# A planner that counts TensorE's instructions in blocks of 256, and a batch's sparse work dealt out anew over the dense stages of the batch before it

## The chip, the core and the metric

The kernel runs on one core of one Trainium2 chip. A core has five engines, each with its own queue that is worked off in order: PE (TensorE: matmuls, and the weight loads that go with them, which the profile shows as PEld), DVE (VectorE), ACT (ScalarE), POOL (GpSimd) and SP (SyncE, which here issues most of the DMAs). The metric is the time on the device in microseconds; less is better.

## The reference

Two stages, for 4 batches, 8 heads, 768 tokens, 64 channels a head. The first is attention under a block mask (blocks of 32 tokens), the second a mixture of four causal attention experts on its output, of which each token takes two.

```python
# stage 1: attention under a block mask, 24 blocks of 32 tokens
scores = scale * np.matmul(q, k.transpose(0, 1, 3, 2))
mask = np.abs(blk_i - blk_j) <= 1                          # neighbours
mask = mask | (blk_i == 0) | (blk_j == 0) | (blk_i == 23) | (blk_j == 23)
for qb in range(24):
    for kb in sampled_blocks[qb]:                          # 3 sampled blocks each
        mask[32*qb:32*qb+32, 32*kb:32*kb+32] = True
attn = softmax(np.where(mask, scores, -1e9)); x = attn @ v # heads joined to 512 channels

# stage 2: four causal attention experts, each token takes the two best
logits = x @ w_gate; w = softmax over the 2 largest
for e in range(4):
    q, k, v = x @ wq[e], x @ wk[e], x @ wv[e]
    ye = causal_softmax(scale * q @ k.T) @ v @ wo[e]
    out += (w of e, 0 where e is not taken) * ye
```

## The kernel before, in words

**Sparse work.** A batch's 768 tokens are six tiles of 128 (four blocks of 32 each). A tile's scores need, for each of its blocks, three neighbouring key blocks, the first and the last block and three sampled ones. `gather_keys` (L581) puts the keys side by side in KK with copies on POOL, ACT or DVE; `gather_values` (L631) does it for the values, into `va` and `vb`, by DMA from a copy of V in HBM (`scr`). Of `va` and `vb` there are two buffers each, taken by even and odd tiles in turn, so tile t's gather can start when tile t-2 has been used. The sampled values take 12 DMAs a tile on SP's queue (L695). `tiles` (L783) then does one half of a tile's heads (a "unit"): scores on PE (L811), row maxima on DVE (L818), exponentials on ACT (L823), transposes on PE (L829), the product with the values on PE (L843, 64 matmuls for each of two pairs of heads), normalisation on DVE, transposes (L860) and the split into `xh` and `xl`. The first and last block of queries attend to all keys: `ends` (L712), twice a batch, works on both together.

For the first batch alone, while nothing else can cover it, two short cuts exist. In `apart` tiles (t < NA) the scores read neighbours and end blocks where they lie (L804, twice the matmuls) and no copies of them are made. And the neighbours and end blocks of the values are copied on POOL from V in SBUF (L642); for the tiles named in `dm` the end blocks come by two DMAs instead (`ends_of`, L650), which here go out from ACT's queue.

**Dense work.** `project_v` (PV, L877; six per batch), `gating` (GT), `project_qk` (PQ, L931), then `expert` (E: scores L972 with a mask by a small matmul L965, maxima L983, exponentials L986, transposes L1022, product L1039) for 2 pairs of experts and 6 row tiles, and `project_o` (O, L1053).

**Order.** No engine's order is written out by hand. The function's end (L1084 to L1092) makes a list `seq` of steps: batch b's dense work is merged, evenly spread, with batch b+1's loads and sparse work, in three stages: the first part of the projections (with tiles 4 and 5 of the same batch and the loads of the next), the second part, and the experts. A step's place in `seq` is its priority. The planner (`Plan.run`, L109) then plays all engines forward with costs that the code gives, and each time an engine is free it takes the ready operation of the best priority. Scores come some steps early: `u`, `e` and `g` say how many for tiles, experts and ends. For PE there is one more rule. The matmuls use the array in different shapes (128 by 128, 64 by 32, 128 by 32 and so on), each operation has its `mode`, and a change of shape costs `SWITCH`; so the planner looks up to `near` steps further for a ready operation of the current shape, and `keep` lets it wait a little for one.

PSUM has two score buffers `s` and four others `w`; the copies out of `w` go to ACT or DVE, whichever the planner finds free.

## Time and profile before

| | |
|---|---|
| timed runs | 524.21, 529.8, 531.16 us; median 529.8 us |
| the profiled execution's own time | 534.0 us |
| its span, from first to last instruction | 532.2 us |
| mean granted clock of PE | 0.987 |
| PE busy | 494.0 us, 93% of the span, 8136 matmuls and 8136 weight loads |
| DVE, ACT, POOL busy | 68%, 63%, 33% |
| share of PE in the chain that ended last | 69% |

Of such a profile one reads first which engine is busy nearly all the time, and then where it is not: a row of the time line with `[2.03 <-issue]` says that the engine stood idle for 2.03 us before this instruction and that nothing which the profile shows (a semaphore, a DMA) released it. In a table by windows each row is a stretch of the span with the busy time of each engine, its instructions, PE's granted clock, and how busy the 16 DMA engines were. The prediction shows the lines.

### The profile page before, as it was taken

To read this page: it belongs to the slowest core of one execution; us is meant where nothing else is said; L and a number is where in the kernel's file an instruction comes from. 1 tells how busy PE (TensorE), PEld (TensorE's weight loads), DVE (VectorE), ACT (ScalarE), POOL (GpSimd) and SP (SyncE) were. 2 spreads that over 40 slices of the span, in tenths; PEclk is the share of its full clock that TensorE was granted. 3 is DMA by queue.
4 is the path that set the end of the run, shared out by engine and by line. 5 is a ranking of instruction groups with operands and counts; after the bars stand their busy time and mean duration, and the time that the engine had idled before them with its cause. 6 is when DMAs were issued, how large, how long until landed. Compare 5 with 4: busy or idle time off the path is not lost.

```text
span 532.2 us, 20854 instructions
## 1 busy us (share of the span) xinstructions
PE 494.0 (93%) x8136; PEld 378.4 (71%) x8136; DVE 364.2 (68%) x980; ACT 333.8 (63%) x936; POOL 177.4 (33%) x446
## 2 busy tenths in 40 slices
PE   2888789897999999998999989999999999999996
PEld 1667477685666777886676758878666778878764
DVE  4867972676897764375978864446988875349783
ACT  2677771575677765484867864556777765435653
POOL 2948742443132350441431332332322321002220
PEclk9989999899999999998999999999999999999999
DMA  7664457987611477976600268867720164000011
GB/s 268 186 163 109 108 143 213 299 208 183 153 30 41 119 222 228 257 181 162 160 26 22 80 154 256 260 154 178 188 65 23 42 161 122 16 2 2 23 41 61
DMA packets 58516, 70.64 MB, mean 133 GB/s; under 512 B 17649, under 2 KB 30065, under 8 KB 58417
## 3 DMA queue, kind: packets, MB, share of 16 engines
q1 hardware_dynamic: 53264, 65.88, 45.9%
q10 hardware_dynamic: 5152, 3.42, 2.2%
q8 instruction: 65, 1.06, 0.9%
q14 instruction: 35, 0.28, 0.2%
HBM read 55.92 MB, written 12.81 MB: 129 GB/s over the span
## 4 chain that ended last, share of the span: by engine, by line
PE 69%; DVE 12%; DMA 5%; ACT 4%; issue 3%; POOL 3%; SPq 2%; POOLq 0%; ACTq 0%; DVEq 0%
PE w L943 10%; PE s L972 7%; PE w L843 7%; PE w L1039 7%; PE w L829 7%; PE w L1022 6%; PE s L811 6%; PE w L1053 6%; PE w L886 6%; DVE sm L983 2%; DMA vb<-scr 2%; POOL va L642 2%; PE s L726 2%; PE w L860 2%; DMA KK<-in_kT_dram 2%
## 5 line engine op out<-in xcount | busy, mean ns | idle before, releaser
L1012 POOL TENSOR_SCALAR p<-p,sm 128x512 f32<-128x512 f32 (+3 forms) x73 | 44.6, 621 | 165.6 <-DVE sm L999 46.5
L469 ACT ACTIVATE pt<-w 128x512 f32<-128x512 f32 (+3 forms) x157 | 81.5, 549 | 22.4 <-PE w L829 9.9
L823 ACT ACTIVATE p<-s,sm 128x256 f32<-128x256 f32 x192 | 78.0, 487 | 16.1 <-DVE sm L818 13.0
L986 ACT ACTIVATE p<-s,sm 128x512 f32<-128x512 f32 (+3 forms) x128 | 68.5, 544 | 24.6 <-DVE sm L983 23.8
L610 POOL COPY KK<-KK 128x128 f32 x231 | 58.2, 298 | 50.2 <-PE s L811 32.3
L473 DVE COPY pt<-w 128x512 f32<-128x512 f32 (+3 forms) x83 | 47.0, 577 | 25.7 <-PE w L829 17.5
L983 DVE TENSOR_REDUCE sm<-s 128x2 f32<-128x1024 f32 (+3 forms) x64 | 54.2, 853 | 11.2 <-PE s L972 10.6
L818 DVE TENSOR_REDUCE sm<-s 128x4 f32<-128x1024 f32 x48 | 57.7, 1214 | 5.6 <-PE s L811 4.4
L829 PE MATMUL w<-ident,p 128*128 128x128 f32 x384 | 54.6, 281 | 7.3 <-ACT p L823 3.8
L829 PEld LDWEIGHTS w<-ident,p 128*128 128x128 f32 x384 | 43.6, 143 | 14.6 <-ACT p L823 5.0
L843 PE MATMUL w<-vb,pt 128*32 128x65 f32 x1536 | 49.5, 220 | 2.9 <-DMA vb<-scr 1.8
L843 PE MATMUL w<-va,pt 128*32 128x65 f32 x1536 | 49.8, 223 | 2.3 <-issue 2.3
L1022 PE MATMUL w<-ident,p 128*128 128x128 f32 x336 | 49.1, 280 | 2.6 <-DVE p L1011 0.9
L972 PE MATMUL s<-qk 64*128 64x512 f32 (+3 forms) x256 | 50.4, 491 | 0.0
L1022 PEld LDWEIGHTS w<-ident,p 128*128 128x128 f32 x336 | 36.7, 141 | 16.9 <-issue 7.9
L1039 PE MATMUL w<-pt,vb 128*64 128x128 f32 x672 | 46.0, 279 | 2.8 <-issue 2.1
L1039 PEld LDWEIGHTS w<-pt,vb 128*64 128x64 f32 x672 | 36.1, 137 | 16.5 <-issue 6.7
L843 PEld LDWEIGHTS w<-va,pt 128*32 128x32 f32 x1536 | 36.6, 109 | 15.4 <-issue 8.6
L943 PE MATMUL w<-xh,wqkh 128*128 128x512 f32 (+1 forms) x128 | 45.6, 356 | 0.3 <-issue 0.3
L811 PE MATMUL s<-KK,q 64*32 64x256 f32 x1280 | 44.4, 382 | 0.3 <-ACT p L823 0.3
L596 ACT ACTIVATE KK<-KK 128x256 f32<-128x256 f32 (+3 forms) x84 | 34.5, 458 | 15.4 <-DMA KK<-in_kT_dram 10.5
L943 PE MATMUL w<-xl,wqkh 128*128 128x512 f32 (+1 forms) x128 | 43.5, 340 | 0.0
(132 smaller groups left out, 996.9 us busy)
## 6 DMA issues: line engine op xcount, KB each, us to landing
vb<-scr SPq DMA_DIRECT2D x270, 65.0 KB, 3.1
va<-scr SPq DMA_DIRECT2D x12, 780.0 KB, 6.2
scr<-VN SPq DMA_DIRECT2D x12, 520.0 KB, 5.4
KK<-in_kT_dram SPq DMA_DIRECT2D x16, 384.0 KB, 5.9
out_dram<-ws SPq DMA_DIRECT2D x24, 256.0 KB, 2.3
ws<-in_v_dram SPq DMA_DIRECT2D x18, 256.0 KB, 3.3
q<-in_qT_dram SPq DMA_DIRECT2D x18, 256.0 KB, 4.9
va<-scr SPq DMA_DIRECT2D x6, 585.0 KB, 5.8
```

What stands on the lines that cost most here:

```text
L469: nc.scalar.activation(dst(), src(), AF.Copy, scale=1.0 if mul is None else mul)
L610: e.tensor_copy(dst, src)
L811: nc.tensor.matmul(s.t[32 * g:32 * g + 32, j, 256 * i:256 * i + 256], q.t[r, pairs[i], 32 * g:32 * g + 32], kg.t[r, i, cl(t, g)].rearrange ...
L823: pl.add("ACT", 0.37, lambda i=i, j=j, n=n: nc.scalar.activation(pp.t[:, 256 * n:256 * n + 256], s.t[:, j, 256 * i:256 * i + 256], AF.Exp, ...
L829: nc.tensor.transpose(w.t[:, 128 * c:128 * c + 128], pp.t[:, 512 * (c // 2) + 256 * i + 128 * (c % 2):][:, 0:128], ident)
L843: nc.tensor.matmul(o.t[32 * g:32 * g + 32, VW * n:VW * n + VW], pt.t[:, 4 * i + 2 * j + c, 32 * g:32 * g + 32], x.t[:, cl(t, g), h * VW:h ...
L943: nc.tensor.matmul(w.t[:, 0:cw], a[:, k, x], y[:, k, c0:c0 + cw], start=n == 0, stop=n == 3 * KT - 1)
L972: nc.tensor.matmul(ss[i].t[:, j, 0:cw], qk.t[x, 0, r * 128:(r + 1) * 128], qk.t[x, 1, c0:c0 + cw], start=not mask_first, stop=mask_first o ...
L983: pl.add("DVE", 0.09 + 0.00208 * cw, lambda i=i, cw=cw: nc.vector.tensor_reduce(sm.t[:, 2 * i:2 * i + 2], ss[i].t[:, :, 0:cw], AX.X, op=AL ...
L986: pl.add("ACT", 0.26 + 0.00083 * cw, lambda i=i, j=j, c0=c0, cw=cw: nc.scalar.activation(pps[j].t[:, p0[j] + c0:p0[j] + c0 + cw], ss[i].t[ ...
L1022: nc.tensor.transpose(w.t[:, 128 * i:128 * i + 128], pps[j].t[:, p0[j] + 128 * t:][:, 0:128], ident)
L1039: nc.tensor.matmul(o.t[64 * j:64 * j + 64, 0:128], vb.t[:, t, e * D:(e + 1) * D], pts[j].t[:, t0s[j] + t], start=t == 0, stop=t == r, tile ...
```

## The change

Five things change together.

1. The planner gets a model of how PE's instructions arrive: PE operations carry their number of instructions (`ni`), `fetching` counts them in blocks of `BLOCK` = 256 and holds that the next block is asked for when a block begins and is at hand `FETCH` us later, or more when many DMAs are queued (`JAM`). An operation that would be late by it costs that much.
2. PE's choice is made anew: all ready operations within `near` steps of the oldest are gathered; one that costs neither a change of shape nor a late block is taken at once, and else the cheapest, with 0.02 for each step of lower priority. `pull` is 0, so that term does nothing. `keep` is empty: PE no longer waits for an operation of its shape.
3. Scores of experts may come 7 steps early (before 4), of ends 4 (before 5).
4. In the first batch, tile 3 is no longer `apart` (`na` 3 for 4), and no end blocks of values come by DMA (`dm` empty for (1,)): tile 1's eight come by POOL copies.
5. The next batch's sparse work is dealt out anew: its ends and tile 0 stand beside the second part of the projections, tiles 1, 2 and 3 beside the experts. Before, tiles 0 and 1 stood beside the second part, and the ends with tiles 2 and 3 beside the experts.

```diff
 SWITCH, DLAT = 0.095, 1.9
+BLOCK, FETCH, JAM = 256, 3.6, 0.15
...
+        count, at_hand = 63.0, {}
+
+        def fetching(o, d, put=False):
+
+            nonlocal count
+            n, late, c = o.ni * 1.02, 0.0, count
+            asked = {}
+            while n and int((c + n) // BLOCK) > int(c // BLOCK) + len(asked):
+                k = int(c // BLOCK) + len(asked) + 1
+                tb = t + late + d * (k * BLOCK - c) / n
+                w = max(0.0, at_hand.get(k, 0.0) - tb)
+                late += w
+                asked[k + 1] = tb + w + FETCH + min(2.5, JAM * max(0.0, dma_free - t - 1.0))
+            if put:
+                count += n
+                at_hand.update(asked)
+            return late
...
-                    if pick is not None and (x[0][0] > pick[0][0] + self.near or all(m[0] != mode for m in o.mode)):
+                    if pick is not None and x[0][0] > oldest + self.near:
...
+                        if e != "PE":
+                            pick = x
+                            break
+                        c = min(SWITCH * ((m[0] != mode) + (m[0] != m[1])) for m in o.mode) + fetching(o, o.dur[0])
+                        if pick is None:
+                            pick, oldest, ready = x, x[0][0], []
+                        ready.append((c, x))
+                        if c == 0.0:
                             break
                         continue
                     skipped.append(x)
+                if pick is not None and e == "PE":
+                    def rank(y):
+
+                        if y[0] == 0.0:
+                            return -1.0
+                        m = y[1][2].mode[0][0]
+                        return y[0] - self.pull * sum(z[1][2].dur[0] for z in ready if z[1][2].mode[0][0] == m) + 0.02 * (y[1][0][0] - oldest)
+
+                    pick = min(ready, key=rank)[1]
+                    skipped += [y[1] for y in ready if y[1] is not pick]
...
-    TUNE = dict(window=24, look=20, near=3, u=7, e=4, g=5, keep={"PE": 0.09}, byact=0, dm=(1,), wat=2)
+    TUNE = dict(window=24, look=20, near=3, u=7, e=7, g=4, keep={}, byact=0, dm=(), wat=2, na=3, pull=0.0)
...
-    NKG, NQ, NA, NC = 3, 4, 4, 6
+    NKG, NQ, NA, NC = 3, 4, TUNE["na"], 6
...
+    MIX = ([4, 5], ['e', 0], [1, 2, 3])
+
+    def tiles_of(b, x):
+        return sum([{"e": ends_(b), "e0": ends_(b)[:1], "e1": ends_(b)[1:]}[t] if isinstance(t, str) else block(b, t) for t in x], [])
+
...
-        seq += merge(first_part(b), block(b, 4) + block(b, 5), [] if last else loads(b + 1))
+        seq += merge(first_part(b), tiles_of(b, MIX[0] if b else [4, 5]), [] if last else loads(b + 1))
         if not last:
-            seq += merge(second_part(b), block(b + 1, 0) + block(b + 1, 1))
-            seq += merge(experts(b), ends_(b + 1) + block(b + 1, 2) + block(b + 1, 3))
+            seq += merge(second_part(b), tiles_of(b + 1, MIX[1]))
+            seq += merge(experts(b), tiles_of(b + 1, MIX[2]))
```

Beside these, each `pl.add("PE", ...)` gets its `ni`: 16 for an ends' score, 48 for its product, 32 (apart 64) and 64 for a tile's, 24 for PV and PQ, 8 or 12 for an expert's score, 8 for each row tile in its product, 12 for O, 2 for each transpose.

Three places in the orders, before and after. Line numbers of the changed kernel are larger by 36 in the second half of the file. First PE, at the end of batch 1's experts, where tile 3 of batch 2 runs (L811, L860, L829 and L843 are the tile's scores, last transposes, transposes and product; L1022, L1039 and L1053 an expert's transposes, its product, and the output projection). Before:

```order
L811 MATMUL s<-KK,q 32x256 x16
L1022 MATMUL w<-ident,p 128x128 x4
L860 MATMUL w<-ident,xn 128x128 x2
L1022 MATMUL w<-ident,p 128x128 x2
L811 MATMUL s<-KK,q 32x256 x8
L1039 MATMUL w<-pt,vb 64x128 x6
L1022 MATMUL w<-ident,p 128x128 x2
L811 MATMUL s<-KK,q 32x256 x8
L1039 MATMUL w<-pt,vb 64x128 x2
```

After:

```order
L1089 MATMUL w<-woh,o 128x512
L896 MATMUL w<-ident,xn 128x128 x2
L1058 MATMUL w<-ident,p 128x128 x2
L865 MATMUL w<-ident,p 128x128 x4
L1058 MATMUL w<-ident,p 128x128 x2
L865 MATMUL w<-ident,p 128x128 x4
L847 MATMUL s<-KK,q 32x256 x16
L1075 MATMUL w<-pt,vb 64x128 x4
L879 MATMUL w<-va_71,pt 32x65 x4
L879 MATMUL w<-vb_73,pt 32x65 x4
```

Before, operations of three array shapes follow each other in pieces of 2 to 16; now the output projection and the transposes stand together, then the scores, then the tile's product, four rows of which follow on those shown.

Second, PE around the product of batch 2's tile 1 with its gathered values (`va_71` and `vb_73` are the odd tiles' buffers; L972 and L965 are an expert's scores and mask). Before, the end of that product:

```order
L843 MATMUL w<-va_71,pt 32x65 x4
L843 MATMUL w<-vb_73,pt 32x65 x4
L972 MATMUL s<-qk 128x512 x2
L972 MATMUL s<-qk 128x256 x2
L965 LDWEIGHTS ident_b
L965 MATMUL s<-tri,ident_b 128x128
L965 LDWEIGHTS ident_b
L965 MATMUL s<-tri,ident_b 128x128
L860 MATMUL w<-ident,xn 128x128 x2
```

After, its beginning:

```order
L1075 MATMUL w<-pt,vb 64x128 x12
L865 MATMUL w<-ident,p 128x128 x4
L1001 LDWEIGHTS ident_b
L1001 MATMUL s<-tri,ident_b 128x128
L1001 LDWEIGHTS ident_b
L1001 MATMUL s<-tri,ident_b 128x128
L1008 MATMUL s<-qk 128x512 x2
L879 MATMUL w<-va_71,pt 32x65 x4
L879 MATMUL w<-vb_73,pt 32x65 x4
```

Before, the product stands ahead of the first scores of batch 1's experts; now it stands behind scores, masks and a product (L1075) of these experts.

Third, ACT in the first batch, around the exponentials of tile 1 (L823, now L859). Before, with the two DMAs of `ends_of`:

```order
L823 ACTIVATE p<-s,sm 128x256 x4
L469 ACTIVATE pt<-w 128x512
L469 ACTIVATE q<-q 128x512
L469 ACTIVATE pt<-w 128x512
L823 ACTIVATE p<-s,sm 128x256 x2
L653 DMA va_71<-VN 32x4x520
L653 DMA vb_73<-VN 32x4x520
L823 ACTIVATE p<-s,sm 128x256 x2
```

After:

```order
L859 ACTIVATE p<-s,sm 128x256 x4
L632 ACTIVATE KK<-KK 128x4x96
L505 ACTIVATE pt<-w 128x512 x2
L859 ACTIVATE p<-s,sm 128x256 x4
L384 TENSOR_LOAD si
L644 ISA
L644 ACTIVATE KK<-KK 128x4x32
```

The two DMAs are gone from ACT's queue; a static copy of tile 3's keys (L632), and behind the exponentials its sampled keys (`TENSOR_LOAD` into registers and L644, 2 times 3 copies), have come into it.

More of the change, by code (lines that the diff above doesn't have):

```diff
@@ L63, with __init__, add @@
 SWITCH, DLAT = 0.095, 1.9
+BLOCK, FETCH, JAM = 256, 3.6, 0.15
 class Op:
[L67 removed]
+    __slots__ = ("eng", "dur", "fn", "prio", "deps", "outs", "n", "slots", "seq", "end", "unit", "lat", "ready", "mode", "xfer", "done", "nd", "ns", "ni")
 class Plan:
[L74 removed]
+    def __init__(self, window, look, near, lat, keep, pull):
         self.ops, self.writers, self.window, self.look, self.near, self.lat = [], {}, window, look, near, lat
[L76 removed]
+        self.keep, self.pull = keep, pull
         self.now = (0, 0)
[L79 removed]
+    def add(self, eng, dur, fn, r=(), w=(), prio=None, unit=None, xfer=None, nd=1, mode=None, ni=0):
         o = Op()
@@ L271, in f @@
         return ap.bitcast(F32)
-    TUNE = dict(window=24, look=20, near=3, u=7, e=4, g=5, keep={"PE": 0.09}, byact=0, dm=(1,), wat=2)
-    pl = Plan(window=TUNE["window"], look=TUNE["look"], near=TUNE["near"], lat={"PE": 0.22, "ACT": 0.17, "DVE": 0.16, "POOL": 0.15, "SP": 0.1}, keep=TUNE["keep"])
+    TUNE = dict(window=24, look=20, near=3, u=7, e=7, g=4, keep={}, byact=0, dm=(), wat=2, na=3, pull=0.0)
+    pl = Plan(window=TUNE["window"], look=TUNE["look"], near=TUNE["near"], lat={"PE": 0.22, "ACT": 0.17, "DVE": 0.16, "POOL": 0.15, "SP": 0.1}, keep=TUNE["keep"], pull=TUNE["pull"])
     def ring(name, n, shape, dt=F32, space=None, ordered=False):
@@ L860, in tiles @@
         pl.add("PE", 0.22, lambda: [nc.tensor.transpose(w.t[:, 128 * i:128 * i + 128], xn.t[:, i], ident)
-                                    for i in range(2)], r=[xn], w=[w, (X[t // 4], "r")], unit=unit, mode=FULL)
+                                    for i in range(2)], r=[xn], w=[w, (X[t // 4], "r")], ni=4, unit=unit, mode=FULL)
         a = 32 if t == 0 else 0
@@ L1054, in mm @@
                     n += 1
-        pl.add("PE", 1.49, mm, r=[(oo, p) for p in range(EP)] + ["wo"], w=[w, (y, "r")], unit=unit, mode=FULL)
+        pl.add("PE", 1.49, mm, r=[(oo, p) for p in range(EP)] + ["wo"], w=[w, (y, "r")], ni=12, unit=unit, mode=FULL)
         evacuate(512, lambda: y.t, lambda: w.t, [w], [y], unit=unit)
```

40 lines of the change are left out of this document (17 added, 23 removed).

## The prediction

> **What bounds the kernel now.** I read the page first, then the stretches by windows, then PE's own idle times.
>
> ```profile
> span 532.2 us, 20854 instructions
> PE 494.0 (93%) x8136; PEld 378.4 (71%) x8136; DVE 364.2 (68%) x980; ACT 333.8 (63%) x936; POOL 177.4 (33%) x446
> PE 69%; DVE 12%; DMA 5%; ACT 4%; issue 3%; POOL 3%; SPq 2%; POOLq 0%; ACTq 0%; DVEq 0%
> ```
>
> PE is busy 494.0 of 532.2 us and carries 69% of the chain. The work on PE hardly changes, so a reordering can win only from the 38 us in which PE stands, from time at a lower clock, and from changes of array shape.
>
> ```profile
> 25.00:50.00 25.00, 20.78 (x698) 17.32 (x703) 18.68 (x50) 19.63 (x53) 16.51 (x35) 0.93 0.55 137
> 50.00:75.00 25.00, 21.68 (x526) 15.80 (x510) 20.76 (x45) 17.53 (x45) 15.53 (x28) 1.00 0.52 124
> 75.00:100.00 25.00, 22.02 (x230) 17.66 (x234) 8.61 (x21) 10.06 (x23) 8.34 (x15) 0.93 0.72 206
> 100.00:125.00 25.00, 22.71 (x511) 18.26 (x507) 17.86 (x48) 16.96 (x43) 11.62 (x39) 1.00 0.89 236
> 225.00:250.00 25.00, 23.23 (x485) 18.63 (x484) 16.51 (x45) 15.66 (x42) 7.95 (x28) 0.93 0.76 178
> 300.00:325.00 25.00, 22.85 (x390) 17.29 (x389) 14.88 (x45) 17.17 (x52) 10.61 (x31) 0.93 0.66 177
> 350.00:375.00 25.00, 25.00 (x508) 20.77 (x508) 16.37 (x44) 17.27 (x47) 6.83 (x24) 1.00 0.67 163
> 375.00:400.00 25.00, 24.43 (x375) 17.45 (x374) 22.26 (x61) 18.45 (x53) 9.01 (x21) 1.00 0.46 116
> ```
>
> The columns are length, busy time of PE, PEld, DVE, ACT, POOL, then PE's clock, the DMA engines' share, GB/s. Up to 100 us (the first batch) PE misses 3 to 4 us of every 25. Later it is full but for three stretches, and two of those also have a clock of 0.93. What PE waits for, in order of time:
>
> ```profile
> 24.12 0.30 PE L804 MATMUL s<-KK,q 64*32 64x64 f32 x4 [1.09 <-issue]
> 48.69 0.25 PE L843 MATMUL w<-vb,pt 128*32 128x65 f32 x2 [1.16 <-issue]
> 124.14 0.22 PE L843 MATMUL w<-va,pt 128*32 128x65 f32 x1 [2.03 <-issue]
> 243.19 0.27 PE L843 MATMUL w<-vb,pt 128*32 128x65 f32 x2 [0.64 <-DMA vb<-scr]
> 244.59 0.24 PE L843 MATMUL w<-vb,pt 128*32 128x65 f32 x1 [1.13 <-DMA vb<-scr]
> 316.22 0.44 PE L1039 MATMUL w<-pt,vb 128*64 128x128 f32 x4 [2.15 <-issue]
> 346.94 0.50 PE L943 MATMUL w<-xh,wqkh 128*128 128x512 f32 x1 [0.32 <-issue]
> ```
>
> Five of them have no releaser ("issue"): no semaphore, no data. They sit in the middle of an operation. What they share is the count of instructions just before:
>
> ```profile
> q8 instruction: 65, 1.06, 0.9%
> 117.40:121.80 4.40, 4.40 (x140) 3.69 (x128) 3.75 (x9) 4.40 (x13) 2.69 (x11) 1.00 1.09 229
> 309.60:313.80 4.20, 4.20 (x130) 2.82 (x127) 3.45 (x13) 3.67 (x14) 2.89 (x8) 1.00 1.02 223
> 343.40:345.70 2.30, 2.30 (x130) 2.11 (x129) 1.72 (x5) 0.96 (x3) 2.14 (x10) 1.00 1.10 359
> ```
>
> PE's 16272 loads and matmuls, some 2% more with waits, over 65 packets of a queue named "instruction" are 255 to a packet. And the three stretches ahead of the later stalls each hold 257 to 268 loads and matmuls, in 4.4, 4.2 and 2.3 us. From the start of such a stretch to PE's return (124.14, 316.22, 346.94) it took 6.7, 6.6 and 3.5 us, each time with the DMA engines full (share above 1). So I read these stalls as a block of 256 being used up before the next has come.
>
> The Trainium skill, page "Runtime: NRT & Kernel Launch", section "Instruction fetch mechanics", says that instructions are refilled in 16 KiB blocks of 256, and that the cost of crossing a block is mostly hidden. The size agrees with the 65 packets of 1.06 MB. That it is hidden does not agree with 6.4 us of idle time in the rows above; taken at its word it makes the counter worthless, which is the second rival below.
>
> **The change, part by part.** The sum is made against the profiled execution's 534.0 us (span 532.2 and 1.8 around it).
>
> *Blocks, batches 1 to 3.* I went through both orders of PE by 256 instructions with durations from the trace. Before, outside the first batch, blocks of 4.3, 3.7, 4.7, 4.1, 4.1, 2.0 and 3.6 us stand there; the new order has one under 5 us (4.4, near the end, where few DMAs run). The 2.03, 2.15 and 0.32 us go: -4.5 us. Blocks of 5.0 to 5.8 us remain, about ten, under the 6.6 of the crowded cases; if three of them wait 1.2 us each, only -0.9 is left.
>
> *Blocks, first batch.* Before 2.4, 3.1, 2.0, 4.1, 2.5, 3.2, 3.5; now 3.4, 3.1, 2.0, 3.9, 2.7, 4.1, 4.5. Tile 3 sends 128 instructions fewer. Of 1.09 and 1.16 us I take half: -1.1 us (0 to -2.3).
>
> *The gathered values.* Odd buffers of `va` and `vb` were free when batch 1's tile 5 was done at 228.11; then SP had to issue the sampled rows of batch 2's tile 1:
>
> ```profile
> 227.06 1.05 PE w L843 x64
> 231.72 11.30 SPq L695 DMA_DIRECT2D vb<-scr  x12
> vb<-scr SPq DMA_DIRECT2D x270, 65.0 KB, 3.1
> ```
>
> 231.72 + 11.30 is 243.0, and landing comes on top: PE, 14 us after the release, was too early. In the new order the ends, tile 0 and the first expert work stand ahead of that product, and the PE work between the same two points is about 37 us by the trace's durations. The smallest such distance of any tile in batches 1 to 3 rises from 14 to 19 us, against the roughly 15 that SP and the landing take. -1.8 us (0.64 + 1.13). Of the three tiles now beside the experts each still has its 12 DMAs in SP's queue, ahead of outputs that nobody waits for.
>
> *The clock.* Two of the stalls are followed by a stretch at half clock:
>
> ```profile
> 317.70:321.00 3.30, 3.30 (x18) 2.34 (x11) 2.01 (x6) 3.04 (x10) 2.25 (x9) 0.50 0.60 192
> 246.10:249.30 3.20, 3.20 (x16) 2.04 (x13) 2.31 (x4) 0.51 (x2) 0.62 (x1) 0.50 1.10 246
> ```
>
> Half of 3.3 and 3.2 us: -3.2 us when both stalls go. The stall of 2.03 us at 124.14 had no such stretch, so this is not certain to the execution; 0 is the other end.
>
> The Trainium skill, page "TensorE: Matmul & The Clock Gate", section "HAM oscillation — how this bites in real kernels", puts the rule at no PE idle gaps above about 3.4 us. Here the clock fell after 2.15 us; by that rule it should not have, and the sum would be 3.2 us higher (about 523). I go by the rows.
>
> *Changes of shape.* Counted on the orders, neighbouring operations of PE differ in shape 322 times before and 304 times now, though `keep` no longer waits for one. What one costs:
>
> ```profile
> 353.43 1.89 PE s L811 x64
> 421.59 1.02 PE s L811 x32
> ```
>
> The second 32 matmuls cost 0.87, so each run of a shape has about 0.15 us on top. 18 times 0.10 (part of it is the pipeline's own) is -1.8 us; 0.9 to 2.7.
>
> *First batch's copies.* `dm` puts eight more copies on POOL, and tile 3's keys are now laid out:
>
> ```profile
> L642 POOL COPY va<-VN 32x520 f32<-32x520 f32 (+2 forms) x53 | 34.3, 648 | 21.1 <-DVE sm L733 10.0 <-PE w L843 8.5
> 38.23 0.53 POOL L610 COPY KK<-KK 128x128 f32 x2 [5.74 <-ACT p L823]
> 31.98 0.86 ACT L608 ACTIVATE KK<-KK 128x128 f32 x3 [1.90 <-DMA vb<-scr]
> 33.47 0.71 ACT L608 ACTIVATE KK<-KK 128x128 f32 x3 [0.63 <-issue]
> ```
>
> 8 times 0.648 is 5.2 us on POOL, which fits the 5.74 that POOL stood idle just there: nothing, and 5.2 without that cover. Two sampled sets on ACT take 4.1 us with their waits (0.63 + 0.71 + 0.86 + 1.90), with tile 2's last exponentials queued behind, which PE's transposes wait for; POOL and the two DMA issues are freed of as much. ACT has 5.4 us free in 25 to 50 us. I take +1 us; -1 if the saved DMAs count, +4 if all of it shows.
>
> *New waits.* Some are sure to come where none was, ends beside gating for one. I take +1.5 us, about one more wait like those at 243; 0 to 7.
>
> Sum: 534.0 - 4.5 - 1.1 - 1.8 - 3.2 - 1.8 + 1.0 + 1.5 = 524.1 us for an execution like the profiled one. That one is 4.2 us above the median of the timed runs (529.8); taken off, 519.9 us.
>
> What stays: PE's wait of 2.1 us between 75 and 100 us, on the copies of `qk` that stand in ACT's and DVE's queues behind copies of keys whose load has not landed. In the new order as many of these copies stand there.
>
> ```profile
> PE w L829 <- DVE qk L475: 2.1, 1, 2.1
> ```
>
> **The rivals.**
>
> *DVE becomes the bound beside the second part (slower).* The ends' work on DVE, four times:
>
> ```profile
> L733 DVE TENSOR_REDUCE sm<-s 128x2 f32<-128x1024 f32 (+1 forms) x16 | 15.1, 952 | 5.8 <-PE s L726 5.5
> L764 DVE TENSOR_TENSOR ws<-w,sm 128x260 f32<-128x260 f32 x8 | 3.4, 425 | 1.6 <-PE w L754 0.9 <-POOL KK L610 0.7
> L768 DVE TENSOR_TENSOR ws<-ws,sm 128x128 f32<-128x128 f32 x8 | 3.2, 396 | 0.3
> ```
>
> is (15.1 + 3.4 + 3.2) / 4 = 5.4 us a batch, some 7 with the small ones. It moves beside gating, whose result every expert needs. If all of it lay open at the three transitions, with a stretch at half clock each time (1.6): 519.9 + 3 x 8.6 = 546 us. It decides from 3.3 us a transition on, where the 10 us of gain are gone. Against it: DVE has 7 to 9 us free in the stretches of the second part (17.86, 16.51, 16.37 of 25), tile 1's work leaves them, and it is the experts' stretch that is full (22.26 of 25), which gets lighter.
>
> *The stalls without a releaser are not blocks of instructions (little gain).* Then the counter moves them at best: 4.5, 1.1 and 1.6 us of clock stay, 527 us. Against it stand the three counts near 256.
>
> *As many waits come as go.* The planner's costs are its own, and PE's order is fixed before the run. Wherever an exponential or a copy is later than planned, PE stands. With one wait of 243's kind in each of the three batches beyond what I took (1.8 + 1.6 of clock), 530 us: no change.
>
> *More than these stalls goes.* If the first batch loses half of the 3 to 4 us that PE misses in each 25 as well, 8 us less: 512 us.
>
> **How the numbers follow.** Chances: the forecast with its own range, 515 to 525, 0.51; more goes 0.16; as many come as go 0.20; not blocks 0.07; DVE the bound 0.06. The likeliest gives 519.9. The costs' open ends reach from 512 (the last rival, about the lower bounds together) to 530 (the third), and outside 510 to 531 I leave no more than 2 in 10. About 2% is what a measurement of this kernel can tell from no change: below 519.2 is faster. That takes a little under half of the forecast (0.24) and the last rival (0.16), with 0.02 from elsewhere: 0.42. Above 540.4 lies the larger part of the DVE rival: 0.05. The rest, 0.53, is within.
>
> **What would show it.** In the changed kernel's trace: no idle time "issue" above 1 us on PE after 100 us (blocks); no wait of PE for `vb<-scr` in batch 2 (gather); a granted clock of 1.00 in every stretch after 100 us; the stretches 25 to 75 us with PE at 21 to 22 as before (first batch); DVE under 22 of 25 in every stretch. If "issue" stalls stand where blocks are long, the count is wrong; if PE waits for DVE's maxima or gating at the transitions, the first rival is right; if PE's busy time falls by more than 3 us, I have mis-sized the changes of shape.

## The result and the profile after

| | before | changed | ratio (95% interval) |
|---|---|---|---|
| first comparison, median of 4 runs each | 529.3 us | 511.9 us (511.2 to 512.2) | 0.968 (0.962 to 0.975) |
| once more beside the last three experiments, 7 and 4 runs | 527.3 us | 513.3 us (511.9 to 513.5) | 0.974 (0.971 to 0.977) |

The changed kernel is faster by 14 to 17 us. The forecast was 519.9, with 510 to 531 as its range. The profiled execution of the changed kernel took 512.2 us. That of the kernel before took 534.0 us and was one of its slow ones, 4.7 to 6.7 us over the two medians, so what is read below from the two traces (21.8 us between them) is more than the gain of the medians. The changed kernel's page, with the span, the busy times and the shares of the chain of waits:

```profile
span 510.4 us, 20714 instructions
PE 484.3 (95%) x8072; PEld 373.7 (73%) x8072; DVE 372.0 (73%) x992; ACT 327.3 (64%) x936; POOL 183.4 (36%) x450
PE 83%; DVE 9%; ACT 3%; DMA 2%; issue 2%; ACTq 0%; POOL 0%; DVEq 0%; POOLq 0%
```

PE's share of the chain rose from 69% to 83%, and DMA, POOL and SP's queue have nearly left it. The stretches of the changed kernel by windows (length, busy time of PE, PEld, DVE, ACT, POOL, then clock, DMA share, GB/s):

```profile
0.00:75.00 75.00, 55.46 (x1356) 39.39 (x1357) 58.31 (x137) 48.59 (x129) 52.99 (x111) 0.93 0.56 158
25.00:50.00 25.00, 20.07 (x625) 16.00 (x623) 20.91 (x49) 18.71 (x53) 22.91 (x41) 0.93 0.49 122
50.00:75.00 25.00, 21.22 (x500) 14.33 (x499) 21.55 (x46) 19.37 (x55) 16.73 (x30) 0.93 0.51 118
75.00:100.00 25.00, 25.00 (x360) 20.53 (x363) 12.52 (x30) 12.03 (x27) 6.50 (x15) 1.00 0.84 247
125.00:150.00 25.00, 24.90 (x440) 18.03 (x438) 23.53 (x62) 19.32 (x60) 11.09 (x28) 1.00 0.55 139
...
75.00:500.00 425.00, 422.70 (x6686) 330.03 (x6687) 311.22 (x846) 275.58 (x799) 129.53 (x338) 1.00 0.51 135
```

And the kernel before, in the same two parts (up to 75 us, and from there to 10 us before the end):

```profile
0.00:75.00 75.00, 55.79 (x1436) 42.51 (x1436) 54.92 (x135) 46.82 (x118) 45.52 (x103) 0.98 0.59 165
75.00:522.00 447.00, 431.98 (x6656) 331.48 (x6656) 306.68 (x840) 284.25 (x811) 130.56 (x342) 0.99 0.48 129
```

Up to 75 us PE stands 19.2 us before and 19.5 us now: nothing gained there. From 75 us on it stood 15.0 us before and stands 2.3 us now, at full clock throughout. So in these two traces the time came from that part alone, and PE is now full there. Three of the waits that PE still has in the first batch (a wait of 0.80 us at 28.8 and one of 2.62 us for ACT at 34.5 stand beside them), and the kind of wait that comes back in each batch behind it, in the changed kernel's timeline:

```profile
48.93 0.62 PE L847 MATMUL s<-KK,q 64*32 64x256 f32 x2 [0.76 <-issue]
54.56 0.27 PE L879 MATMUL w<-vb,pt 128*32 128x65 f32 x2 [0.82 <-issue]
58.73 0.41 PE L896 MATMUL w<-ident,xn 128*128 128x128 f32 x2 [1.72 <-DVE sm L889]
161.92 0.33 PE L1075 MATMUL w<-pt,vb 128*64 128x128 f32 x2 [0.40 <-DVE pt L509]
```

To split the gain I gave each of PE's operations the time that it takes up to the next one where nothing waits (the same kind of operation followed by the same kind, elsewhere in the two traces). By that measure the work itself went from 466.9 to 464.8 us, and all that lies on top of it (waits and lower clock) from 52.3 to 32.5 us. These two, 2.1 and 19.8 us, make up the 21.8 us between the spans. Every "work" and "on top" below is of this kind, worked out from the traces. The sum is firm, the split is not: with the shortest time of each kind as the measure the work falls by 3.5 us, with the mean of those without idle time behind them by 5.7 us. A plain account of the same two traces is PE's idle time, 12.1 us less; the clock, 1.6 us less lost (13.4 and 10.2 us of PE's busy time lie at half clock); and PE's busy time without the clock's part, 8.1 us less (487.3 and 479.2 us).

### The profile page after: what moved, and what is told of

Read it like the earlier page. It is cut to its first block, busy times and chain, and to the rows that moved or that the text cites. A ratio compares the mean times of both kernels' runs of the same rounds, so it can differ in the third digit from the quotient of the medians.

```text
span 510.4 us, 20714 instructions
## 1 busy us (share of the span) xinstructions
PE 484.3 (95%) x8072; PEld 373.7 (73%) x8072; DVE 372.0 (73%) x992; ACT 327.3 (64%) x936; POOL 183.4 (36%) x450
## 4 chain that ended last, share of the span: by engine, by line
PE 83%; DVE 9%; ACT 3%; DMA 2%; issue 2%; ACTq 0%; POOL 0%; DVEq 0%; POOLq 0%
PE w L979 14%; PE w L879 9%; PE w L865 8%; PE s L1008 8%; PE s L847 8%; PE w L1075 7%; PE w L922 7%; PE w L1058 6%; PE w L1089 6%; PE w L896 2%; PE s L762 2%; DVE sm L854 2%; PE w L780 2%; PE w L790 2%; DMA pt<-in_v_dram 2%
## 5 line engine op out<-in xcount | busy, mean ns | idle before, releaser
L859 ACT ACTIVATE p<-s,sm 128x256 f32<-128x256 f32 x192 | 78.1, 485 | 13.6 <-DVE sm L854 8.2
L1022 ACT ACTIVATE p<-s,sm 128x512 f32<-128x512 f32 (+3 forms) x128 | 68.2, 544 | 27.3 <-DVE sm L1019 21.0
L505 ACT ACTIVATE pt<-w 128x512 f32<-128x512 f32 (+3 forms) x134 | 67.5, 530 | 21.6 <-PE w L865 12.1
L509 DVE COPY pt<-w 128x512 f32<-128x512 f32 (+3 forms) x106 | 63.2, 614 | 24.2 <-PE w L865 17.3
L854 DVE TENSOR_REDUCE sm<-s 128x4 f32<-128x1024 f32 x48 | 58.0, 1215 | 12.7 <-PE s L847 12.4
L879 PE MATMUL w<-va,pt 128*32 128x65 f32 x1536 | 48.6, 224 | 0.3 <-issue 0.3
L879 PE MATMUL w<-vb,pt 128*32 128x65 f32 x1536 | 47.6, 221 | 0.8 <-issue 0.8
L847 PE MATMUL s<-KK,q 64*32 64x256 f32 x1344 | 46.9, 388 | 1.1 <-issue 1.1
L1075 PE MATMUL w<-pt,vb 128*64 128x128 f32 x672 | 43.8, 277 | 1.6 <-DVE pt L509 1.6
L879 PEld LDWEIGHTS w<-va,pt 128*32 128x32 f32 x1536 | 35.5, 110 | 13.1 <-issue 6.4
L1075 PEld LDWEIGHTS w<-pt,vb 128*64 128x64 f32 x672 | 36.1, 137 | 12.2 <-issue 3.2
L678 POOL COPY va<-VN 32x520 f32<-32x520 f32 (+2 forms) x57 | 36.7, 645 | 20.2 <-DVE sm L769 10.1
L979 PE MATMUL w<-xh,wqkl 128*128 128x512 f32 (+1 forms) x128 | 43.3, 339 | 0.0
```

Source lines behind the costliest of these rows:

```text
L505: nc.scalar.activation(dst(), src(), AF.Copy, scale=1.0 if mul is None else mul)
L509: nc.vector.tensor_copy(dst(), src())
L847: nc.tensor.matmul(s.t[32 * g:32 * g + 32, j, 256 * i:256 * i + 256], q.t[r, pairs[i], 32 * g:32 * g + 32], kg.t[r, i, cl(t, g)].rearrange ...
L854: pl.add("DVE", 1.16, lambda: nc.vector.tensor_reduce(sm.t[:, 0:4], s.t.rearrange("p j (t c) -> p (j t) c", t=2), AX.X, op=ALU.max, negate ...
L859: pl.add("ACT", 0.37, lambda i=i, j=j, n=n: nc.scalar.activation(pp.t[:, 256 * n:256 * n + 256], s.t[:, j, 256 * i:256 * i + 256], AF.Exp, ...
L879: nc.tensor.matmul(o.t[32 * g:32 * g + 32, VW * n:VW * n + VW], pt.t[:, 4 * i + 2 * j + c, 32 * g:32 * g + 32], x.t[:, cl(t, g), h * VW:h ...
```

## The experiments

Two kinds of kernel were run: the changed kernel with one part taken back, and the kernel before with one or two parts alone. No run takes back the new choice among ready operations (part 2) by itself, and the leads go together with `keep`. Ratios are against the kernel before, timed beside them (527.6 us for the first four rows of experiments, 526.9 for the mix alone, the counter alone and the shifted ones, 527.3 for the rest).

| kernel | us | ratio (95% interval) | changes of shape | PE idle after 75 us | longest stall without a releaser after 75 us |
|---|---|---|---|---|---|
| before (trace: the execution of 534.0 us) | 529.3 | 1 | 322 | 15.0 | 2.15 |
| changed | 511.9 | 0.968 (0.962 to 0.975) | 304 | 2.3 | none |
| changed, counting off | 517.0 | 0.979 (0.973 to 0.985) | 301 | 5.3 | 2.57 |
| changed, old mix | 532.1 | 1.006 (1.003 to 1.010) | 305 | 17.2 | 3.28 |
| changed, old first batch | 517.5 | 0.981 (0.975 to 0.986) | 303 | 5.8 | 2.34 |
| changed, old leads | 524.6 | 0.996 (0.993 to 0.998) | 312 | 8.7 | 1.76 |
| before, new mix alone | 525.2 | 0.995 (0.992 to 0.998) | 302 | 10.6 | 2.33 |
| before, counter alone | 532.2 | 1.009 (1.005 to 1.013) | 328 | 10.1 | 1.74 |
| before, mix and leads | 520.6 | 0.988 (0.985 to 0.991) | 306 | 8.7 | none |
| before, borders shifted | 530.7 | 1.013 (1.004 to 1.022) | 322 | 14.5 | 2.95 |
| changed, borders shifted | 517.5 | 0.982 (0.977 to 0.987) | 304 | 3.9 | 0.74 |
| changed, once more | 513.3 | 0.974 (0.971 to 0.977) | 304 | 2.5 | none |
| changed, 5.5 us a block, old first batch | 517.2 | 0.982 (0.979 to 0.985) | 304 | 4.3 | none |
| changed, 4.5 us a block | 516.4 | 0.978 (0.974 to 0.982) | 301 | 4.6 | 1.11 |

The idle times are from 75 us to about 10 us before the end. A time over another by more than its row explains is mostly in the clock, in the work itself, or ahead of 75 us.

### Are the stalls blocks of instructions?

The direct test leaves every engine's order as it is and moves only the borders of the blocks, by half a block:

```diff
         def sc(i, c0, cw):
+            for _ in range(32 * (b == 0 and pp_ == 0 and i == 0)):
+                nc.tensor.matmul(ss[0].t[0:64, 0, 0:1], ident[0:64, 0:64], ident[0:64, 0:1], start=True, stop=True, ...)
             for j in range(2):
```

> The kernel before, order of every engine unchanged, with 32 products of one column (128 instructions) ahead of the first score product, which overwrites what they wrote; so every later block border falls half a block earlier in the same work. Blocks theory: the stalls of 2.03, 2.15 and 0.32 us leave the operations at which they stood (the 256 instructions up to each now take 5.5 us and more); new ones, if any, stand where 256 instructions pass in 4.3 to 4.5 us (near 191, 205, 228, 363 and 436 us), all at whole multiples of 256 in the count with 128 more. 525 to 530 us. Rival (the stalls belong to these operations, by their shape or their data): they stay at the same operations, 530 to 533 us with the work added.

The kernel before with its borders shifted, PE's timeline:

```profile
124.14 0.32 PE L846 MATMUL w<-va,pt 128*32 128x65 f32 x1 [2.95 <-issue]
311.37 0.77 PE L1042 MATMUL w<-pt,vb 128*64 128x128 f32 x10
340.83 0.40 PE L946 MATMUL w<-xh,wqkh 128*128 128x512 f32 x1
359.93 0.44 PE L832 MATMUL w<-ident,p 128*128 128x128 f32 x2 [2.05 <-issue]
```

The second and the third row hold the operations ahead of which PE stood 2.15 and 0.32 us (the program's `pt,vb` product and key projection); it now goes through them without a pause. A new stall stands at 359.93, where the order had a stretch of 256 in 4.4 us (forecast: near 363; at the other four places named there is none). In the first batch stalls of 1.68, 1.41 and 1.40 us have come where two of 1.09 and 1.16 us were. The time, 530.7 us, is the rival's number; it is the places that speak against the rival, not the time. The stall near 124 us has the same time by chance, but stands 130 loads and matmuls further on in the program (before at the 4225th, here at the 4483rd, of which 128 are added): again at the end of a block. That a stall would come there was not foretold. I had read 5.5 us for that block off the trace of before, with the old stall of 2.03 us in it; here its 256 instructions take 3.3 us from border to border. The same 128 instructions in the changed kernel:

> The changed kernel with the same 128 instructions ahead, order of every engine unchanged, so that its planner's count is half a block off. Theory A (after 75 us the order has so few dense stretches that the place of the borders hardly matters): 512 to 515 us, with at most one stall of 1 to 2 us near 217 us, where 256 instructions now pass in 2.5 us. Theory B (the count's phase is what keeps the stalls away): 517 us and more, several stalls without a releaser after 100 us.

It took 517.5 us, theory B's number, but after 75 us its trace is that of theory A: one stall above 0.5 us, at the foretold place, but of 0.74 us (219.4). The first batch holds most of the rest: PE has stalls of 1.26, 0.82 and 2.08 us there, and two stretches of 6.8 us at half clock. So with this one shift the changed order after 75 us depends little on where the borders lie, but in the first batch it does.

Over all 14 traces, PE has 36 idle times of 0.6 us and more without a releaser. With PE's loads and matmuls times 1.02, plus 63, over 256 (the planner's own count), 35 of the 36 stand 0.00 to 0.11 above a whole number. In these 35 stalls the 16 KB packet of the queue named "instruction" ends 1.22 to 1.60 us before PE goes on; in the odd one (0.64 us, at 9.25 blocks) 1.96 us. That settles the question for this kernel: PE stands because its next block comes late.

Whether a dense stretch stalls goes with the DMA engines. Three kernels send the same 251 loads and matmuls, in the same order, through the block that ends near 218 us, and all take 2.6 us for it. By windows (the last two columns are the DMA share and GB/s), first the kernel before with mix and leads, no stall behind it:

```profile
215.80:218.40 2.60, 2.60 (x125) 2.43 (x127) 1.08 (x4) 1.20 (x2) 0.00 (x0) 1.00 0.27 74
```

Then the changed kernel with shifted borders, 0.74 us behind it:

```profile
215.70:218.30 2.60, 2.60 (x122) 2.43 (x124) 1.07 (x4) 1.20 (x2) 0.00 (x0) 1.00 0.53 130
```

Then the kernel before with the mix alone, 2.33 us:

```profile
215.50:218.10 2.60, 2.60 (x122) 2.42 (x124) 1.06 (x4) 1.20 (x2) 2.22 (x10) 1.00 1.07 235
```

And two other blocks, of the kernel before with the counter alone, 1.74 us behind the first, none behind the second:

```profile
308.40:311.70 3.30, 3.30 (x127) 2.25 (x134) 2.96 (x8) 2.93 (x12) 1.45 (x6) 1.00 1.01 311
334.50:336.80 2.30, 2.30 (x130) 2.09 (x129) 1.71 (x7) 1.48 (x4) 1.87 (x8) 1.00 0.09 16
```

The same instructions stall not at all with the engines at 0.27, a little at 0.53 and most at 1.07. Read in this way over all traces after 75 us, a block that passed in less than 4.5 us was followed by a stall of 0.3 us or more at 10 of 11 places with a share above 0.97 (at the eleventh PE waited for DVE just then), and at 1 of 37 places with less. No run changed the traffic alone, so these are cases beside each other and not a test.

### What the counter is worth

```diff
-BLOCK, FETCH, JAM = 256, 3.6, 0.15
+BLOCK, FETCH, JAM = 10 ** 9, 3.6, 0.15
```

> The changed kernel with a block so large that none is ever used up, so the planner counts nothing; table and mix as changed. PE's order then differs only in the first batch and at one place near 115 us. Theory A (the counter earned the gain of the first batch's stalls, the mix the rest): stalls without a releaser of 1 us and more come back before 75 us and nowhere else, 513 to 515 us against 511.9. Theory B (the counter is the change, its avoided stalls carry most of the 17 us): over 520 us, with stalls without a releaser after 100 us.

The changed kernel without counting, PE's timeline and the window behind the stall:

```profile
103.39 0.31 PE L879 MATMUL w<-vb,pt 128*32 128x65 f32 x6 [2.57 <-issue]
```

```profile
104.40:107.80 3.40, 3.40 (x22) 2.39 (x15) 2.73 (x5) 1.29 (x4) 2.43 (x7) 0.50 0.62 209
```

5.1 us slower than the changed kernel's first median, 3.7 us slower than its second, and the intervals of the ratio overlap (0.973 to 0.985 against 0.971 to 0.977 for the second); the trace shows what the time alone would not. Neither theory had the place right. The orders differ only up to about 115 us. The counter did not thin out the first batch (0.98 us there without it, 0.76 and 0.82 with it); it took apart one dense stretch beside the second part of batch 0, where the stall and the half clock behind it make 100 to 125 us longer by 4.3 us. The disappeared stalls of 124, 316 and 347 us owe it nothing: they are gone in this kernel too (the largest that is left behind 104 us is 0.42 us, at another border, 315 us).

The counter alone (with the new choice among ready operations), written as the changed kernel with the old table and mix:

```diff
-    TUNE = dict(..., e=7, g=4, keep={}, ..., dm=(), ..., na=3, ...)
+    TUNE = dict(..., e=4, g=5, keep={"PE": 0.09}, ..., dm=(1,), ..., na=4, ...)
-    MIX = ([4, 5], ['e', 0], [1, 2, 3])
+    MIX = ([4, 5], [0, 1], ['e', 2, 3])
```

> The kernel before with the counter and the new choice among ready operations alone; old table, old mix. 328 changes of shape instead of 322. Theory A (with the old mix the counter can't get round the dense stretches: 256 instructions still pass in 2.0 and 3.4 us at two places): 526 to 531 us, the wait for vb<-scr and the 2.1 us wait stay. Theory B (the counter is what takes the stalls away): 519 to 523 us, no stall without a releaser over 1 us after 100 us.

PE's timeline:

```profile
314.02 0.37 PE L847 MATMUL s<-KK,q 64*32 64x256 f32 x1 [1.74 <-issue]
```

532.2 us, no gain and a little loss (0.9%): theory A's side, 1.2 us above its range. PE's work, by the measure above, grew by 2.0 us. A stall of 1.74 us stands near 314; the other dense stretch, near 337, did not stall (both windows are shown above). The two waits that theory A kept, for the gathered values in batch 2 and of 2.1 us for `qk`, are gone.

Would a planner that reckons more for a block do better? Both tries were slower than the changed kernel. First:

```diff
-BLOCK, FETCH, JAM = 256, 3.6, 0.15
+BLOCK, FETCH, JAM = 256, 4.5, 0.15
```

> The changed kernel with 4.5 us for a block in the planner instead of 3.6; 301 changes of shape, and by the order one stretch near 103 us in which 256 instructions pass in 2.5 us, as in the kernel with the counting off. Theory A (such a stretch beside full DMA engines stalls, whatever the planner reckons): a stall of 2 to 3 us without a releaser near 103 us, a stretch at half clock behind it, 514 to 517 us. Theory B (a larger figure for a block gives a better order): 510 to 512 us, no such stall.

The changed kernel with 4.5 us a block, PE's timeline:

```profile
102.90 0.31 PE L879 MATMUL w<-vb,pt 128*32 128x65 f32 x5 [1.11 <-issue]
```

516.4 us: the stall is where theory A put it, but only 1.11 us, without a stretch at half clock; a further one of 2.23 us stands at 71 us in the first batch.

Then 5.5, with the old first batch:

```diff
-BLOCK, FETCH, JAM = 256, 3.6, 0.15
+BLOCK, FETCH, JAM = 256, 5.5, 0.15
-    TUNE = dict(..., dm=(), wat=2, na=3, ...)
+    TUNE = dict(..., dm=(1,), wat=2, na=4, ...)
```

> The changed kernel with the first batch as before (na=4, dm=(1,)) and a planner that reckons 5.5 us for a block instead of 3.6. By the order the 256 instructions ahead of the place of the 2.34 us stall near 88 us are no longer a dense stretch; 304 changes of shape. Theory A (undoing the first batch's part cost time only by that one stall and its half clock, 4 us): 511 to 514 us, no stall without a releaser over 1 us after 75 us, first batch with 1 to 2 us less idle than in the changed kernel. Theory B (the first batch's part earns time by itself): 516 us and more without such a stall.

With 5.5 us a block and the old first batch, PE's timeline:

```profile
56.53 0.69 PE L865 MATMUL w<-ident,p 128*128 128x128 f32 x2 [3.88 <-ACT p L859]
70.11 0.32 PE L879 MATMUL w<-va,pt 128*32 128x65 f32 x8 [2.21 <-ACT pt L505]
```

517.2 us, and theory A is wrong: there is no stall without a releaser after 75 us, as it said, but the first batch lost time instead of winning it, to data that ACT has not made yet. Theory B has the number, though this run does not show its reason, since the planner's figure was changed along with the first batch.

### What the mix is worth

```diff
-    MIX = ([4, 5], ['e', 0], [1, 2, 3])
+    MIX = ([4, 5], [0, 1], ['e', 2, 3])
```

> The changed kernel with the old mix (tiles 0 and 1 beside the second part, the ends and tiles 2 and 3 beside the experts); counter and table as changed. Theory A (the mix carries the gain after 75 us: gathered values, qk copies behind key copies, the waits at the transitions): 521 to 527 us; the wait of 2.1 us between 75 and 100 us and a wait for vb<-scr in batch 2 are back. Theory B (counter and table carry it): 512 to 515 us, no such waits.

The changed kernel with the old mix, PE's timeline:

```profile
122.73 0.25 PE L879 MATMUL w<-va,pt 128*32 128x65 f32 x3 [3.28 <-issue]
131.41 0.88 PE L847 MATMUL s<-KK,q 64*32 64x256 f32 x24 [1.91 <-ACT p L1022]
338.34 0.32 PE L879 MATMUL w<-va,pt 128*32 128x65 f32 x8 [1.70 <-ACT pt L505]
359.92 0.58 PE L865 MATMUL w<-ident,p 128*128 128x128 f32 x2 [2.54 <-issue]
```

532.1 us: all of the gain is lost, and more than theory A allowed. The time on top of the work is 19.0 us higher and the work 1.3 us, which is the 20 us. But the waits are not those that theory A named: none for `vb<-scr`, none for `qk` at 95 us. They are new stalls of blocks (3.28 and 2.54 us, each with a half clock) in spite of the counter, and waits for ACT. With tiles 0 and 1 beside the second part, the planner found no good order here.

The same mix alone in the kernel before:

```diff
-            seq += merge(second_part(b), block(b + 1, 0) + block(b + 1, 1))
-            seq += merge(experts(b), ends_(b + 1) + block(b + 1, 2) + block(b + 1, 3))
+            seq += merge(second_part(b), ends_(b + 1) + block(b + 1, 0))
+            seq += merge(experts(b), block(b + 1, 1) + block(b + 1, 2) + block(b + 1, 3))
```

> The kernel before with the new mix alone (ends and tile 0 beside the second part, tiles 1 to 3 beside the experts); no counter, old table. Theory A (the mix carries the gain after 75 us): 514 to 519 us; no wait for vb<-scr in batch 2, no wait of 2.1 us for qk between 75 and 100 us, though nothing counts blocks. Theory B (without the counter the mix only moves the stalls): 524 to 530 us, with stalls without a releaser after 100 us, most likely where 256 instructions pass in 2.7 us (near 205 us) and in 3.5 us (near 475 us).

PE's stall and the window behind it:

```profile
220.83 0.30 PE L843 MATMUL w<-vb,pt 128*32 128x65 f32 x2 [2.33 <-issue]
```

```profile
221.20:224.60 3.40, 3.40 (x21) 1.46 (x19) 2.28 (x5) 0.09 (x1) 0.00 (x0) 0.50 0.85 216
```

525.2 us, theory B's number, 0.5% better than before (0.992 to 0.998). The waits that theory A named are gone, as it said, but a stall of 2.33 us with its half clock stands near 221 us, some 16 us behind the first of theory B's two places; at the second there is none.

### What the leads are worth

```diff
-    TUNE = dict(..., e=7, g=4, keep={}, ...)
+    TUNE = dict(..., e=4, g=5, keep={"PE": 0.09}, ...)
```

> The changed kernel with the old leads: e=4, g=5 and keep for PE at 0.09; counter, mix and first batch as changed. 312 changes of shape instead of 304. Theory A (the leads only move changes of shape): 0.8 to 1.2 us more, 513 us. Theory B (the longer lead of the experts' scores is what took the small waits at the stages' borders away, 3.8 us in all before): 515 to 518 us, with waits of 0.6 to 1.4 us at 130, 143, 152 us and the like.

The changed kernel with the old leads, two windows and PE's timeline:

```profile
125.00:150.00 25.00, 23.33 (x358) 15.98 (x358) 22.91 (x61) 20.52 (x62) 10.40 (x27) 1.00 0.60 145
350.00:375.00 25.00, 22.52 (x424) 19.11 (x408) 18.26 (x53) 18.07 (x51) 7.44 (x25) 1.00 0.41 96
```

```profile
354.43 0.45 PE L790 MATMUL w<-VN,pt 128*64 128x65 f32 x7 [1.76 <-issue]
```

12.7 us slower, over both forecasts. The work is 1.6 us longer (with 8 more changes of shape) and 10.2 us more lies on top. A stall of a block at 354 us makes 1.76 of it; the rest is spread in pieces of 0.25 to 1.1 us over all batches, most of them in the experts' part (the window at 125 us, where PE stands 1.7 us). So theory B has the direction, and one more block has come on top.

Mix and leads together, in the kernel before (the mix as just shown, and):

```diff
-    TUNE = dict(..., e=4, g=5, keep={"PE": 0.09}, ...)
+    TUNE = dict(..., e=7, g=4, keep={}, ...)
```

> The kernel before with the new mix and the new leads (e=7, g=4, keep empty), without counter and with the old first batch. 306 changes of shape; by the order one stretch near 219 us in which 256 instructions pass in 2.7 us. Theory A (mix and leads together do what neither does alone, and what is left to the changed kernel is one or two stalls with their half clock): 516 to 520 us, a stall of 2 to 3 us near 219 us. Theory B (without the counter mix and leads gain nothing, as the mix alone): 524 us and more.

PE's timeline in that kernel:

```profile
142.38 0.33 PE L1022 MATMUL w<-ident,p 128*128 128x128 f32 x1 [1.07 <-POOL p L1012]
...
383.27 0.33 PE L1022 MATMUL w<-ident,p 128*128 128x128 f32 x1 [1.09 <-POOL p L1012]
```

520.6 us, 0.6 us above theory A's range: 6.7 us gained, where the mix alone gained 1.8. The stall near 219 us that it foretold did not come (the DMA share was 0.27 there, as shown above). What is left to the changed kernel is 7.3 us (513.3 in the same comparison): 9.0 us more lies on top of the work in its trace, in which a wait of 1.1 us for POOL in each batch is the most regular.

### The first batch

```diff
-    TUNE = dict(..., dm=(), wat=2, na=3, ...)
+    TUNE = dict(..., dm=(1,), wat=2, na=4, ...)
```

> The changed kernel with the first batch as before (four tiles with scores from two places, dm=(1,)); counter, mix and the leads as changed. Theory A (the first batch's part of the change cost time, 1.7 us more idle time on PE up to 75 us than before): 509.5 to 511 us. Theory B (it freed SP and POOL so that the loads of 75 to 100 us land earlier, which took the 2.1 us wait away): 514 to 517 us, that wait back.

The changed kernel with the old first batch, PE's timeline:

```profile
87.66 0.30 PE L879 MATMUL w<-vb,pt 128*32 128x65 f32 x3 [2.34 <-issue]
```

517.5 us, 5.6 us slower. The saving of theory A is there (up to 75 us 2.0 us less on top of the work than in the changed kernel), the 2.1 us wait for `qk` of theory B is not; the time is nearer to B's, half a microsecond above it. But a block border now lies behind a dense stretch at 88 us, and the stall with its half clock makes 75 to 100 us 4.1 us longer. Of the 4.3 us between the two traces' spans the other 2.2 lie in small pieces.

The changed kernel itself, beside the last three:

> The changed kernel itself, once more, beside the next three. Both theories: 511 to 513 us.

513.3 us, a little over the forecast. None of the other kernels beat it.

### Why the wait at 95 us went

The prediction let a wait of 2.1 us between 75 and 100 us stand. Three traces of the same place. Before:

```profile
94.15 0.44 ACT L596 ACTIVATE KK<-KK 128x288 f32<-128x288 f32 x1 [1.13 <-DMA KK<-in_kT_dram]
94.42 0.68 DVE L475 TENSOR_SCALAR qk<-w 128x512 f32<-128x512 f32 x1
```

The kernel before with its borders shifted, that is, with the same order:

```profile
91.95 0.45 ACT L596 ACTIVATE KK<-KK 128x288 f32<-128x288 f32 x1 [0.87 <-DMA KK<-in_kT_dram]
92.22 0.68 DVE L475 TENSOR_SCALAR qk<-w 128x512 f32<-128x512 f32 x1
94.85 1.04 PE L832 MATMUL w<-ident,p 128*128 128x128 f32 x8
```

The changed kernel:

```profile
89.47 0.75 ACT L632 ACTIVATE KK<-KK 128x288 f32<-128x288 f32 x2 [1.07 <-DMA KK<-in_kT_dram]
90.29 0.69 DVE L511 TENSOR_SCALAR qk<-w 128x512 f32<-128x512 f32 x1 [0.20 <-PE w L979]
93.33 1.04 PE L865 MATMUL w<-ident,p 128*128 128x128 f32 x8
```

The copy of `qk` stands behind the same copies of keys in all three. In the second the last load of keys lands 2.2 us sooner than in the first, with no change of order, and PE comes to the transposes with nothing to wait for. The wait is gone in every one of the experiments' traces. So the order alone does not make this wait: it came of a race between a load and PE. How often executions of the kernel before lose that race is not shown, since only one was traced. The wait for the gathered values is different: it stands in both traces of that order, 1.77 us before and 0.87 us at 243.6 us with the borders shifted.

## Why the prediction was right, and where it was not

The range held the time, the direction was right, and the size was short: 9.9 us of gain forecast against the 529.8 us median, 17.4 and 14.0 us measured. In the terms of its sum, 524.1 us was forecast for the profiled execution and 512.2 came. The likeliest case, 515 to 525 us, did not come, and a change that a measurement can tell was given less (0.42) than none (0.53). That the wider range held is in part luck: what made the gain larger is not in the sum.

**Blocks, batches 1 to 3 (-4.5): right in size, not owed to the counter.** The three stalls are gone, none came in their place, and they were blocks: 35 of 36 stalls agree. But with the counting off those three are gone as well; the counter paid elsewhere, at 103 us, where about 4.3 us lie. I had also read the lengths of blocks off traces with stalls in them, as the shifted kernel showed.

The Trainium skill's page "Runtime: NRT & Kernel Launch", section "Instruction fetch mechanics", which has the cost of crossing a block as mostly hidden, fits the changed kernel after 75 us and not the kernels with stalls there, in which single crossings cost up to 3.28 us. The rival worked out from it, that the counter would be worth nothing, falls with the stall at 103 us that came back without it; in the kernel before the counter alone did earn nothing.

**The gathered values (-1.8): right.** No wait of PE for `vb<-scr` in batch 2 of the changed kernel. The mix is enough for it (in the kernel before with the mix alone the wait is gone) but not needed, since with the old mix and the rest of the change it was gone too.

**The clock (-3.2): right after 75 us.** It stands at 1.00 there. The three half-clock stretches of the first batch in the profiled execution cost next to nothing: the second profile of the changed kernel had one such stretch and a span of 510.1 against 510.4 us.

**Changes of shape (-1.8): open.** By the first measure above there is 2.1 us less work, the size that I gave. But the sign that I named for a wrong size came, PE's busy time falling by more than 3 us: it fell by 9.7, of which the clock makes 1.6. The number of changes does not carry that. The mix alone has 302 of them and 1.4 us less busy time without the clock's part than before; the changed kernel has 304 and 8.1 us less. That time is 485.9 to 487.6 us in the five kernels which lack the new choice among ready operations or the new leads, and 479.2 to 482.8 us in all with both (the two with 128 instructions added aside). A short wait behind a matmul whose end is modelled can count as busy, so the runs do not tell whether this is less work or fewer short waits.

**First batch (-1.1 for blocks, +1.0 for copies): the sum near, the step not.** By idle time the first 75 us cost as much as before (19.5 against 19.2), by the measure above 1.7 us more. POOL did take the copies in, at 22.91 of 25 us.

**New waits (+1.5): failed, the wrong sign.** Waits at the stages' borders went instead of coming. Before, in PE's timeline:

```profile
131.76 0.27 PE L965 MATMUL s<-tri,ident_b 128*128 128x128 bf16 x2 [1.36 <-ACT p L823]
143.22 0.30 PE L1022 MATMUL w<-ident,p 128*128 128x128 f32 x1 [0.61 <-DVE p L1011]
152.23 0.27 PE L965 MATMUL s<-tri,ident_b 128*128 128x128 bf16 x2 [0.61 <-ACT p L986]
295.48 0.33 PE L1022 MATMUL w<-ident,p 128*128 128x128 f32 x1 [0.67 <-DVE xl L486]
383.21 0.27 PE L965 MATMUL s<-tri,ident_b 128*128 128x128 bf16 x2 [0.57 <-ACT p L986]
```

These make 3.8 us, and the changed kernel has none over 0.4 us in the middle of the program. I had read only the largest waits and reckoned the new ones by what might come, without adding up the small ones that stand at places which the change rebuilds. The experiments put them to mix and leads together: the leads taken back bring pieces of this size, and mix and leads alone leave the one for POOL and two of about 0.7 us.

**What stays (2.1 us at 95 us): failed.** It went, and half of its 3.4 us at half clock with it; the whole stretch from 75 to 100 us has 4.5 us less on top. I reasoned from the order of the queues, which was right, but took the landing of a load in one execution for fixed.

With these three (3.8, 4.5 and the 1.5 that never came) 9.8 of the 11.9 us between 524.1 and 512.2 are named. Of the rest, about 1.3 us is less waiting towards the end and some 2.5 us lies in small pieces, against 1.8 us that the first batch took beyond its forecast. This is the account by the first measure. By the plain one the idle time fell by 12.1 us where the sum has 4.9, the clock's loss by 1.6 where it has 3.2, and the busy time without the clock's part by 8.1 where it has 1.8; so up to 6 us of the miss may belong to the term for changes of shape.

**The 4.2 us taken off for the profiled execution: right, if anything short.** The two profiled executions lie 21.8 us apart, the medians 17.4 us, and 14.0 us in the second comparison.

**The rivals.** DVE did fill up beside the experts (23.53 of 25 us at 125 to 150 us, over the 22 I had set as a limit), yet PE lost 0.1 us there: the limit was wrong, not the kernel. "More than these stalls goes" gave 512 us, the right number, from the first batch, which is the wrong place. As for "as many waits come as go": it is what happens to nearly every neighbour of this change. Taking back one part costs 5.1, 20.2, 5.6 or 12.7 us against 511.9 (1.4 us less each against 513.3), some 44 us in all where the whole change earns 14 to 17; and two parts alone, mix and counter, earn 1.8 us and lose 5.2. A time for this change could not be had as a sum over its edits. Why just this order has no dense stretch beside full DMA engines after 75 us, and most of the others do, is not explained by these runs beyond their block borders and waits as listed.

## What to carry to other kernels

Where small matmuls fill PE, count its instructions in blocks of 256 and look for a block that passes in 2 to 5 us while the DMA engines are full: here such borders cost up to 3.3 us, more with the clock that falls behind them, and putting half a block of tiny instructions ahead (here 32 products, 128 instructions) is a cheap test of it. Parts of a change to an order that is fixed beforehand are not terms of a sum: run the whole order, and each part's removal, before giving a part a price. A wait on a load that lands just too late in one profiled execution may be a race; see whether another execution, or the same order a little later, has it too, before calling it something that stays.

## What the runs showed of the hardware

- PE goes on 1.22 to 1.60 us after the packet with its next block of instructions has been moved, in 35 stalls of 12 different kernels. The same block of 251 loads and matmuls, in 2.6 us, was followed by no stall at a DMA share of 0.27, by 0.74 us at 0.53 and by 2.33 us at 1.07.
- The clock halved for 3.4 us (two windows above) behind stalls of 2.15, 2.33, 2.34, 2.54, 2.57, 2.95 and 3.28 us after 75 us; it did not behind 2.03 us (before, at 124 us), nor behind 2.05 us (the first window below, the kernel before with borders shifted), nor behind 2.23 us at 71 us (the second, the changed kernel with 4.5 us a block). A page of the Trainium skill, "TensorE: Matmul & The Clock Gate", section "HAM oscillation — how this bites in real kernels", has the limit at gaps above about 3.4 us; every one of these stalls is shorter. Nor is the length of one stall what decides: the clock halved too at 246 us in the kernel before, behind waits of 0.64 and 1.13 us, and at 181 us in the kernel before with the counter alone, behind 0.43 and 0.62 us. In each trace these stretches begin whole multiples of 3.41 us apart (before: at 34.4, 95.8, 246.0 and 317.7 us). The windows behind the stalls of 2.05 and 2.23 us:

```profile
360.00:363.40 3.40, 3.40 (x71) 3.21 (x75) 0.91 (x5) 2.30 (x6) 0.00 (x0) 1.00 0.34 84
```

```profile
71.30:74.70 3.40, 3.40 (x38) 3.31 (x30) 1.92 (x6) 1.65 (x4) 3.19 (x5) 1.00 0.72 185
```

- A stall of 2.3 to 2.6 us with the half clock behind it costs 4.1 to 4.6 us in all (75 to 100, 100 to 125 and 200 to 225 us in three kernels, by the measure of "on top").
